# Attention and a squared-ReLU MLP on one core: first products by seven for more chunks, other loads of q and v, and a new written order

## The chip, the cores and the metric

The kernel runs on one core of one Trainium2 chip. The metric is device time in microseconds (us), from the start of the program to its end, as the median of several runs. One execution was also taken by the hardware profiler; its instructions, waits and transfers are the trace that is quoted here. Engines: PE (TensorE, matrix products; PEld is its weight load, which overlaps PE), DVE (VectorE), ACT (ScalarE), POOL (GpSimd), SP (SyncE, which here only issues transfers).

## The reference

For 8 batches and 8 heads, 576 tokens and head width 64, q attends to 16 beacon keys and then, causally, to k; the softmax times the values gives 64 columns a head. The 8 heads side by side are a token's 512 columns, and all 4608 tokens go through an MLP:

```python
scores = scale * np.matmul(q, k_all.transpose(0, 1, 3, 2))   # k_all: 16 beacons, then k; causal after them
a = np.exp(scores - max); a /= a.sum(-1, keepdims=True) + 1e-09
x = np.matmul(a, v_all)                  # -> 4608 x 512
h = x @ w_in                             # 512 x 2048
g = np.maximum(h, 0.0) ** 2
out = g @ w_out                          # 2048 x 512
```

## The kernel before

**Attention**, per batch of 576 tokens and pair of heads (pair p = 4 x batch + number). Batches 0 and 1 are loaded by GpSimd and turned by PE. From batch 2 on, q, k and v come in tiles of up to 128 tokens through SP's queue into six staging buffers `stg` as float32 (`ldBxC`: batch B, tensor x, tile C; `add_load`, lines 370 to 412), are cast by GpSimd (`castBxC`, line 342) into `qb`, `kb` (two buffers each in `qk_area`) or into the value tiles `vb`, and q and k are turned by one transposing transfer each (`trBq`, `trBk`, line 418) into `qT`, `kT`. In such a tile each partition holds one token of all heads, so pieces of 256 bytes are read. `qk...` (line 631) makes the scores of 512 columns at a time: in two PSUM pairs of banks (`strip`) and, where three pieces go together, in two of the four single banks `ps`. ACT takes the exponential into `pt` (`exp`, lines 653 and 729), DVE masks the diagonal blocks (`mask`, line 750, a minimum with `tri`), PE multiplies by the values with a column of ones (`av`, line 771), and DVE divides (`norm`, lines 788 and 790) into `xn`. `xn` is turned into `xT`, a ring of 1728 tokens: by PE for batches 0 to 2 (line 839), by transposing transfers on SP after that (`xt`, line 822).

**The MLP** works on nine chunks of 512 tokens. The first product (`s1.J...`) makes 2048 hidden rows of a chunk J in bf16 in `g[J % 2]`, the second (`s2.J...`) its 512 output columns.

- First product, chunks 0 to 6: 16 groups of 4 matmuls of 512 columns (line 1073), each drained by a relu on ACT or DVE (lines 1088, 1090), and squares in place by pairs of groups (`sq`, lines 1098, 1100). Where a chunk wraps in the ring (chunks 3 and 6), each matmul is cut in two.
- First product, chunks 7 and 8 (`BOTH = 7`, `add_first_both`, line 950): weights and tokens are cut into two halves each (even and odd tokens), and seven products of sums of the quarters take the place of eight (Winograd's scheme). GpSimd first copies the chunk out of the ring (`pull`), DVE makes the sums of the weights once (`asum`) and the differences of x per chunk (`xsum`, line 930). A PSUM bank pair runs through products 1, 6, 7 and 4; between them its content is copied to SBUF (`h...c1`, `u2`, `u3`), and DVE adds these copies to the other products (`c11`, `c22`, `c12`, line 997). Then come a relu in place and the square.
- Second product, chunks 0 and 1: plain, 128x512 (line 1123). Chunks 2 to 8: seven products (line 1182), with sums of g made by DVE (`sumJ.N.I`, line 1154) in three areas of `sum_area`, copies to `osb` (`ev`, line 340 or 342) and adds (line 1205). Results go out through SP.

**The order** of all this is not left to a scheduler: every operation is added to a list with its dependencies, and `SEQUENCE` (lines 16 to 147) names them one by one, with `@A`, `@D` or `@P` for the engine where there is a choice. Each engine runs its own operations strictly in that order, and PSUM banks, staging buffers and `held` areas are taken from pools as they come free. So an operation that waits holds up all that stands behind it on its engine.

Of the kernel before, what the change touches and what calls it, by code (L numbers as in the profile page):

```python
# [12 lines left out]
BIG = 3.0e38  # L13
# [3 lines left out]
ident tri fldq0 fldk2 fldq1 bkl0 fldq2 fldk1 warm sld0k1.0 fldk0 sld0q1.0 fcq0 sld0k1.2 tp0.0.0q eq0.0.0@D sld0q1.2  # L17
fck2 tpg0.0.0q fck3 tp0.0.2k fcq1 ld0v0 bkc0 tp0.0.3k ek0.0.2@A ek0.0.3@D tpg0.0.2k tpb0 tpg0.0.3k tp0.0.1q ekb0
fcq3@A fcq2@D ld0v1 bkl1 eq0.0.1@A tp0.0.3q fck1 tpg0.0.1q tp0.0.2q ld0v2 eq0.0.3@A eq0.0.2@D qk3.0.0 tpg0.0.3q ld0v3
tpg0.0.2q tp0.0.1k tp0.1.0k exp3.0.0 fck0 ld0v4 qk2.0.0 ek0.0.1@D ek0.1.0@D tpg0.0.1k tp0.0.0k exp2.0.0 win0 qk1.0.0  # L20
mask3.0.0 tpg0.1.0k tp0.1.0q ek0.0.0@A mask2.0.0 exp1.0.0 qk0.0.0 tpg0.0.0k win2 tp0.1.2k eq0.1.0@A mask1.0.0 exp0.0.0
ek0.1.2@D qk0.1.0 tpg0.1.0q tp0.1.1q tpg0.1.2k win1 exp0.1.0 mask0.0.0 qk0.1.1 cast0v0@D tp0.1.1k exp0.1.1 eq0.1.1@D
qk0.1.2 mask0.1.1 win3 tpg0.1.1q tp0.1.2q ek0.1.1@A cast0v1@D exp0.1.2 eq0.1.2@D qk1.1.0 tpg0.1.1k bkc1 av0.0.0
tpg0.1.2q av1.0.0 sld1k0.0 exp1.1.0 mask0.1.0 tp0.1.3k norm0.0.0 qk2.1.0 cast0v2 tpb1 ek0.1.3@D qk1.1.1 exp2.1.0 ekb1
cast0v3 av2.0.0 norm1.0.0 tpg0.1.3k xtp0.0.0 exp1.1.1 tp0.1.3q xte0.0.0@D qk1.1.2 sld1q0.0 eq0.1.3@D xtp0.0.1 av3.0.0
exp1.1.2 norm2.0.0 tpg0.1.3q qk3.1.0 cast0v4 norm3.0.0 xtp0.0.2 exp3.1.0 sld1k0.2 qk2.1.1 mask1.1.0 av0.1.0 mask1.1.1
mask2.1.1 exp2.1.1 sld1q0.2 mask3.1.1 av1.1.0 xte0.0.1@A norm0.1.0 ld1v0 xte0.0.2@A xtp0.0.3 mask2.1.0 qk2.1.2
xte0.0.3@A norm1.1.0 xtp0.1.0 exp2.1.2 s1.0.1.0 xte0.1.0@D s1.0.3.0 relu0.1.0@D qk3.1.1 ld1v1 relu0.3.0@A s1.0.11.0
exp3.1.1 av2.1.0 relu0.11.0@D mask3.1.0 xtp0.1.1 s1.0.0.0 norm2.1.0 xte0.1.1@A s1.0.2.0 relu0.0.0@D qk3.1.2 ld1v2
relu0.2.0@A sq0.0.0@D xtp0.1.2 sq0.1.0@A s1.0.6.0 xte0.1.2@D exp3.1.2 s1.0.8.0 relu0.6.0@D s1.0.9.0 relu0.8.0@D  # L30
s1.0.10.0 relu0.9.0@A av3.1.0 sq0.4.0@D relu0.10.0@A ld1v3 sq0.5.0@D s1.0.12.0 norm3.1.0 s1.0.4.0 relu0.12.0@A
s1.0.5.0 relu0.4.0@A ld1v4 tp1.0.0k relu0.5.0@A xtp0.1.3 sq0.2.0@A ek1.0.0 s1.0.13.0 s1.0.14.0 xte0.1.3@A relu0.13.0@D
wout0 tpg1.0.0k tp1.0.0q relu0.14.0@A sq0.6.0@D s1.0.11.1 eq1.0.0@D tp1.0.1k relu0.11.1@A s1.0.8.1 wout1 tpg1.0.0q
ek1.0.1 tp1.0.1q relu0.8.1@A qk4.2 tpg1.0.1k eq1.0.1@D tp1.0.2k wout2 exp4.2.0.0.0 s1.0.15.1 tpg1.0.1q ek1.0.2
tp1.0.3q exp4.2.1.0.0 s1.0.12.1 wout3 tpg1.0.2k eq1.0.3@D s1.0.5.1 relu0.12.1@A mask4.0.0 qk4.4 tpg1.0.3q relu0.15.1@A
relu0.5.1@D cast1v0 s1.0.2.1 exp4.4.0.0.0 tp1.0.2q cast1v1 relu0.2.1@D s1.0.14.1 eq1.0.2@D exp4.4.1.0.0 cast1v2
s1.0.13.1 relu0.14.1@D s1.0.0.1 tpg1.0.2q relu0.13.1@A cast1v3 mask4.0.2 mask4.0.1 qk5.7 sq0.7.1@A sq0.6.1@D cast1v4
relu0.0.1@A s1.0.1.1 exp5.7.-1.1.0 s1.0.9.1 relu0.1.1@D exp5.7.-1.0.0 av4.0.0 relu0.9.1@D exp5.7.1.0.0 s1.0.10.1
mask5.0.0 norm4.0.0 av4.0.1 relu0.10.1@A s1.0.7.1 sq0.4.1@A mask5.0.2 norm4.0.1 s1.0.3.1 sq0.5.1@A relu0.7.1@D
tp1.0.3k sq0.0.1@A xtp1.0.0 ek1.0.3 relu0.3.1@A s1.0.4.1 xte1.0.0@A s1.0.6.1 zero2 tpg1.0.3k relu0.4.1@D sq0.1.1@A  # L40
s1.0.15.0 wsum1 sq0.2.1@A s1.0.7.0 zero3 s2.0.0.0 relu0.15.0@A relu0.7.0@A relu0.6.1@D exp5.7.0.0.0 sq0.3.0@D s2.0.2.0
sq0.3.1@D sq0.7.0@D qk7.13 mask5.0.1 s2.0.0.1 exp7.13.-1.1.0 exp7.13.-1.0.0 av5.0.0 exp7.13.0.0.0 s2.0.0.2 norm5.0.0
ld2k0 exp7.13.1.0.0 wsum2 av5.0.1 s2.0.0.3 ld2q0 norm5.0.1 s2.0.3.0 ev0.0@A ld2q1 mask7.0.1 mask7.0.2 xtp1.0.1 ld2q2
s2.0.3.1 xte1.0.1@A cast2k0 ld2q3 s2.0.2.1 qk6.10 cast2q0 ld2k1 s2.0.2.2 exp6.10.0.0.0 cast2q1 ld2q4 s2.0.3.2
exp6.10.1.0.0 s2.0.2.3 exp6.10.-1.1.0 mask6.0.1 cast2q2 ld2k2 mask6.0.2 exp6.10.-1.0.0 s2.0.3.3 exp6.10.1.0.1 ev0.2@D
cast2q3 ld2k3 mask6.0.0 s2.0.1.0 ev0.3@A mask7.0.0 av6.0.0 cast2k1 st1 av7.0.0 norm6.0.0 ld2k4 cast2q4 s2.0.1.1
norm7.0.0 av6.0.1 cast2k2 tr2q av7.0.1 norm6.0.1 s2.0.1.2 norm7.0.1 cast2k3 xtp1.0.2 xtp1.0.3 xte1.0.2@D s2.0.1.3
xte1.0.3@A s1.1.1.0 ev0.1@A cast2k4 st0 s1.1.2.0 relu1.1.0@A tr2k s1.1.3.0 relu1.2.0@A s1.1.9.0 relu1.3.0@A sq1.1.0@D
s1.1.4.0 relu1.9.0@A s1.1.5.0 relu1.4.0@A ld2v0 s1.1.6.0 relu1.5.0@A sq1.2.0@D s1.1.13.0 relu1.6.0@A ld2v1 s1.1.14.0
ld2v2 relu1.13.0@A s1.1.15.0 relu1.14.0@A s1.1.8.0 relu1.15.0@A ld2v3 sq1.7.0@D qk8.2 relu1.8.0@A s1.1.10.0  # L50
exp8.2.0.0.0 sq1.4.0@D cast2v0 ld2v4 s1.1.11.0 relu1.10.0@D exp8.2.1.0.0 cast2v1 ld3k0 s1.1.0.0 relu1.11.0@A mask8.0.0
qk8.4 sq1.5.0@D relu1.0.0@A cast2v2 ld3q0 s1.1.7.0 exp8.4.0.0.0 sq1.0.0@D s1.1.12.0 cast2v3 ld3q1 exp8.4.1.0.0
# [155 lines left out]
def kernel(  # L208
# [694 lines left out]
    def add_first_both(j, G, sq):  # L903
# [32 lines left out]
        for half in range(2):  # L936
# [58 lines left out]
            def plus(name, chain, n, quad, added, u, last, half=half, bank=bank, done=done, ev=ev, keep=keep, sums=sums):  # L995
# [6 lines left out]
                if u:  # L1002
                    give.append(keep[added])
# [334 lines left out]
```

## Time and profile before

| what | value |
|---|---|
| median of 3 runs | 331.17 us (329.81 to 331.58) |
| span of the profiled execution, first to last instruction | 327.7 us |
| granted PE clock, mean | 1.000 |
| instructions in the trace | 8732 |
| matmuls of line 1073 / 1182 / 950 in the built order | 640 / 784 / 224 |

The profiled execution is given by its span; the times of the runs are whole device times, with a few microseconds around the span. In rows of a group, "x64 | 37.8, 599 | 16.9" means 64 instructions, busy 37.8 us in all, 599 ns a piece on average, and the engine idle for 16.9 us just before them, with what ended that. A matmul's own duration holds its passage through the pipeline; how fast PE really goes is read from the distance of starts, or from the chain, whose pieces (start, length, what) don't overlap. In a row of stretches stand the stretch, its length, the busy time of PE, PEld, DVE, ACT and POOL with counts, the granted clock, the share of the 16 DMA engines and GB/s.

### The profile page before, as it was taken

Reading aid. Unit: us, or ns where it says so; the run is one execution under the profiler, and the core shown is the slowest. Engines: PE = TensorE matmul, PEld = TensorE weight load, DVE = VectorE, ACT = ScalarE, POOL = GpSimd, SP = SyncE. Lnnn points to the kernel's source line nnn. Section 1 sums busy time; section 2 is a strip of 40 time slices with the busy share of each in tenths; the row PEclk is TensorE's granted clock in tenths of the full one; section 3 lists DMA queues with packets and bytes.
Section 4 is the critical chain, followed back from the end, with each engine's and each line's share of the span. In section 5 each row is a group of like instructions: output and inputs, shape, how many; then the busy total and the mean of one; then the engine's idle time right before and its main releaser. Section 6 shows DMA issues by size and latency. Waiting matters only on the chain.

```text
span 327.7 us, 8732 instructions
## 1 busy us (share of the span) xinstructions
PE 315.9 (96%) x3582; PEld 227.6 (69%) x3582; DVE 231.9 (71%) x487; ACT 225.7 (69%) x332; POOL 101.1 (31%) x149
## 2 busy tenths in 40 slices
PE   2999999999999999999999999999999999999995
PEld 1478785544565558888866565776788788888884
DVE  3777886534655899587864788768865797897871
ACT  4867796458874984777766889767837664695931
POOL 9854713404532450424033403641100252000000
PEclk9999999999999999999999999999999999999999
DMA  8999998899999999999999998997913210110033
GB/s 159 220 205 215 206 169 170 168 214 204 205 177 201 240 219 171 178 244 230 180 138 215 221 181 204 202 207 156 225 23 130 46 28 2 69 61 0 2 148 111
DMA packets 145602, 51.98 MB, mean 159 GB/s; under 512 B 132506, under 2 KB 140570, under 8 KB 145562
## 3 DMA queue, kind: packets, MB, share of 16 engines
q1 hardware_dynamic: 135901, 42.32, 65.7%
q0 software_dynamic: 8512, 8.49, 15.4%
q10 hardware_dynamic: 1149, 0.62, 0.9%
q8 instruction: 28, 0.46, 0.6%
q14 instruction: 12, 0.10, 0.1%
HBM read 37.22 MB, written 9.44 MB: 142 GB/s over the span
## 4 chain that ended last, share of the span: by engine, by line
PE 85%; DMA 8%; SPq 1%; ACT 1%; POOL 1%; DVE 1%; issue 1%; ACTq 0%; POOLq 0%; DVEq 0%
PE ps L1073 26%; PE ps L1182 21%; PE ps L771 9%; PE ps L1123 8%; PE strip L631 6%; PE strip L950 4%; PE ps L950 3%; DMA stg<-in_q_dram 3%; PE strip L1182 2%; DMA kT<-qk_area 2%; PE ps L631 2%; DMA osb<-in_q_dram 2%; DMA stg<-in_v_dram 2%; PE ps L839 1%; SPq L822 1%; PE ps L474 1%
## 5 line engine op out<-in xcount | busy, mean ns | idle before, releaser
L1073 PE MATMUL ps<-xT,w_in 128*128 128x512 bf16 (+6 forms) x640 | 106.3, 315 | 0.6 <-ACT pt L729 0.6
L1073 PEld LDWEIGHTS <-w_in 128*128 128x128 bf16 x640 | 56.2, 98 | 34.8 <-issue 1.6
L729 ACT ACTIVATE pt<-strip 128x1024 bf16<-128x1024 f32 (+3 forms) x77 | 69.6, 955 | 7.8 <-PE strip L631 7.7
L1088 ACT ACTIVATE g<-ps 128x512 bf16<-128x512 f32 (+2 forms) x82 | 44.4, 551 | 20.1 <-PE ps L1073 17.2
L342 POOL CAST qk_area<-stg 128x512 bf16<-128x512 f32 (+2 forms) x60 | 39.9, 672 | 53.7 <-DMA stg<-in_k_dram 31.5
L342 POOL CAST vb<-stg 128x512 bf16<-128x512 f32 (+1 forms) x38 | 27.4, 728 | 83.6 <-DMA stg<-in_v_dram 69.4
L750 DVE TENSOR_TENSOR pt<-pt,tri 128x512 bf16<-128x512 bf16 (+1 forms) x93 | 37.8, 424 | 16.1 <-ACT pt L729 14.8
L1182 PEld LDWEIGHTS <-g 128*128 128x128 bf16 x448 | 42.9, 98 | 7.0 <-issue 0.8
L771 PEld LDWEIGHTS <-pt 128*128 128x128 bf16 x930 | 35.8, 100 | 7.0 <-issue 1.2
L771 PE MATMUL ps<-vb,pt 128*128 128x65 bf16 x930 | 38.4, 197 | 0.0
L1182 PE MATMUL ps<-w_out,g 128*128 128x256 bf16 x304 | 38.0, 273 | 0.0
L1090 DVE TENSOR_SCALAR g<-ps 128x512 bf16<-128x512 f32 (+2 forms) x46 | 27.9, 607 | 13.2 <-PE ps L1073 12.6
L1182 PEld LDWEIGHTS <-sum_area 128*128 128x128 bf16 x336 | 32.0, 98 | 5.5 <-issue 1.4
L790 DVE TENSOR_TENSOR xn<-ps,rcp 128x320 bf16<-128x320 f32 (+2 forms) x64 | 31.5, 491 | 2.2
L340 ACT COPY osb<-ps 128x512 f32<-128x512 f32 x26 | 15.2, 586 | 25.2 <-PE ps L1182 19.0
L1123 PE MATMUL ps<-w_out,g 128*128 128x512 bf16 x128 | 31.2, 379 | 0.0
L1100 DVE TENSOR_TENSOR g<-g 128x1024 bf16<-128x1024 bf16 (+2 forms) x35 | 23.4, 673 | 10.6 <-ACT g L1088 9.9
L631 PEld LDWEIGHTS <-kT 64*128 64x128 bf16 x618 | 20.0, 95 | 14.1 <-issue 10.3
L631 PE MATMUL strip<-qT,kT 64*128 64x128 bf16 (+14 forms) x500 | 29.5, 246 | 0.3 <-ACT qT L340 0.2
L1098 ACT ACTIVATE g<-g 128x1024 bf16<-128x1024 bf16 (+2 forms) x29 | 26.7, 941 | 3.0 <-DVE g L1090 2.0
L729 ACT ACTIVATE pt<-ps 128x512 bf16<-128x512 f32 x42 | 23.4, 599 | 5.7 <-PE ps L631 5.6
L1182 PE MATMUL ps<-w_sum,sum_area 128*128 128x256 bf16 x208 | 26.0, 273 | 0.0
(93 smaller groups left out, 357.7 us busy)
## 6 DMA issues: line engine op xcount, KB each, us to landing
out_dram<-osb SPq DMA_DIRECT2D x16, 512.0 KB, 3.8
stg<-in_q_dram SPq DMA_DIRECT2D x24, 256.0 KB, 4.6
stg<-in_k_dram SPq DMA_DIRECT2D x18, 256.0 KB, 5.1
stg<-in_v_dram SPq DMA_DIRECT2D x18, 256.0 KB, 4.6
w_in<-in_moe_w_in_dram POOLq DMA_DIRECT2D x4, 512.0 KB, 12.0
w_out<-in_moe_w_out_dram POOLq DMA_DIRECT2D x4, 512.0 KB, 10.9
stg<-in_v_dram POOLq DMA_DIRECT2D x6, 256.0 KB, 8.0
stg<-in_k_dram SPq DMA_DIRECT2D x6, 224.0 KB, 4.1
```

The lines of the kernel that those rows point to most:

```text
L342: eng[e].tensor_copy(dst, src)
L631: nc.tensor.matmul(out, kT[b % 2][hp, pr, 128 * c:128 * c + 128], rhs, start=True, stop=True)
L729: nc.scalar.activation(out, in_, AF.Exp, bias=0.0, scale=scale)
L750: nc.vector.tensor_tensor(out=d, in0=d, in1=tri[0:rows, m0:m0 + m, 0:w][:, None].to_broadcast([rows, 2, m, w]), op=ALU.min)
L771: nc.tensor.matmul(a[:, at + (t - tl[0]) * (D + 1):at + (t - tl[0] + 1) * (D + 1)], P[0:rr, hj, o:o + 128], vb[b % 2][0:rr, c, 2 * pr + hj ...
L790: nc.vector.tensor_tensor(out=xn[b % 2].rearrange("p t (h d) -> p h t d", d=D)[:, h0:h0 + nh, tl[0]:tl[0] + nt], in0=a[:, :, :, 0:D], in1= ...
L1073: nc.tensor.matmul(h[:, lo - spans[0][0]:hi - spans[0][0]], w_in_sb[:, mc, ft * 128:(ft + 1) * 128], xT[:, mc, lo % RING:lo % RING + hi - lo],
L1088: nc.scalar.activation(dst, h, AF.Relu, bias=0.0, scale=1.0)
L1090: nc.vector.tensor_scalar(out=dst, in0=h, scalar1=0.0, scalar2=None, op0=ALU.max)
L1098: nc.scalar.activation(d, d, AF.Square, bias=0.0, scale=1.0)
L1123: nc.tensor.matmul(o, G[:, fc, ts * 128:(ts + 1) * 128], w_out_sb[:, fc, :], start=(fc == 0), stop=(fc == NFT - 1))
L1182: nc.tensor.matmul(o, lhs[:, f, t * 128:(t + 1) * 128], rhs[:, f], start=fresh and f == 0, stop=f == HF - 1, skip_group_check=True)
```

## The change

- **Chunks 3 to 6 by seven products too** (`BOTH = 3`). The form is another: four units of two row groups each, every bank chain in single `ps` banks; x is read in place from the ring, every other column, without pulls; of the four differences of x, three stand in a small area `spare` and one replaces its operand in the ring. The relu is folded into the adds, by a custom DVE instruction (`TENSOR_ADD_SAT` with bounds 0 and BIG), and into the drain of product 4. The areas that hold the copies are three, in `spare`.
- **The sums of the second product** are made mostly in place in g (`sum 2`, `sum 4` wait for products 1 and 2), with one area `s_sum`; GpSimd may make them.
- **q of batches 2 to 7** is loaded for two heads at a time with four consecutive tokens to a partition (pieces of 1 KB), so that the columns of `qT` come out in another order, and the scores read them with a step of 128, cut at column 512.
- **v of batches 2 to 7** is loaded by GpSimd's queue with a cast straight into `vb`, without staging and without a cast instruction.
- **One buffer** instead of two for `qb` and for `kb`; a cast waits for the transpose of the batch before.
- **Masks** may be made by GpSimd (a select of the diagonal block), casts by ACT or DVE; `tri` is smaller, `bks` lies in `w_sum`.
- A relu now waits for the second product two chunks back, where its matmuls did.
- **A new `SEQUENCE`** throughout, from the first loads on.

```diff
-    FAST, FAST_PE = 2, 0.9
-    BOTH = 7
-    NSTG, NPT, RB = 6, 3, 3
+    FAST, BOTH = 2, 3
+    SOFT = "v"
+    NSTG, NPT, RB, NH = 6, 3, 3, 3
...
+    def add_soft_load(b, x, c, behind):
...
+            insts.append(nc.gpsimd.dma_start(out=dst[lo:rows], in_=t[b, :, t0:t0 + rows - lo, :].transpose([1, 0, 2])))
...
+            if fours:
+                return [queue.dma_start(out=st[0:rows].rearrange("p (u s) d -> p u s d", s=4),
+                                        in_=t[b, 2 * c:2 * c + 2, 0:4 * rows, :].rearrange("u (p s) d -> p u s d", s=4))]
...
+            if b >= NPE:
+                fours = qT[b % 2][hp, pr, 0:512].rearrange("p (s n) -> p n s", s=4)
+                parts = [(x, y, z) for x, y, z in ((t0, min(t1, 512), fours), (max(t0, 512), t1, None)) if x < y]
...
+                if e == "POOL":
+                    for i in range(m):
+                        nc.gpsimd.affine_select(out=d[:, :, i], in_=d[:, :, i], compare_op=ALU.is_ge, fill=0.0,
+                                                base=Nb if m0 + i == 0 else 0, pattern=[[0, 2], [1, w]], channel_multiplier=-1)
+                    return
...
+        def in_ring(c, q):
+            return [xT[:, HM * c:HM * c + HM, lo % RING:lo % RING + hi - lo].rearrange("p m (i q) -> p m q i", q=2)[:, :, q]
+                    for lo, hi in spans]
...
+        for n, o, a, c in ((1, pieces(s[1]), b12, b11), (2, pieces(s[2]), b22, pieces(s[1])), (3, b12, b22, b12),
+                           (4, pieces(s[4]), b21, pieces(s[2]))):
...
+                for i in range(2):
+                        f = 2 * u + i
+                        for part, (at, w) in zip(rhs, where):
+                            for m in range(HM):
+                                nc.tensor.matmul(o[:, i * HT + at:i * HT + at + w], lhs[:, m, f * 128:(f + 1) * 128],
+                                                 part[:, m], start=fresh and i == 0 and at == 0 and m == 0, stop=m == HM - 1,
+                                                 skip_group_check=True)
...
+                    nc.vector._custom_dve(TENSOR_ADD_SAT, out=dst, in0=bank_of(chain),
+                                          in1=held[keep[added].held[1]].rearrange("p (f t) -> p f t", f=2), s0=BIG, s1=0.0)
...
+            product(2, "z", A[0, 1], b21, cuts, feeds + weights)
+            product(1, "x", A[0, 0], b11, cuts, feeds + weights)
+            hold("c1", 1)
+            plus("c11", "z", 2, block(0, 0), "c1", True)
+            product(5, "y", a_sum[1], [s[1]], one, a_ops[1] + x_ops[1])
+            product(6, "x", a_sum[2], [s[2]], one, a_ops[2] + x_ops[2] + ev["c1"])
+            hold("u2", 6)
+            product(7, "x", A[1, 0], b12, cuts, a_ops[3] + x_ops[3] + ev["u2"])
+            hold("u3", 7)
+            plus("c22", "y", 5, block(1, 1), "u3", False)
+            product(4, "x", A[1, 1], [s[4]], one, x_ops[4] + ev["u3"])
+            last("c21", 4, block(1, 0))
+            product(3, "y", a_sum[4], b22, cuts, a_ops[4] + ev["c22"])
+            plus("c12", "y", 3, block(0, 1), "u2", True)
```

585 lines of the change are left out of this document (285 added, 300 removed).

## The prediction

> **What bounds the kernel now.** I read the page's busy times first, then the busy times of engines by stretch, then the chain that ended last, then the groups by shape.
>
> ```profile
> span 327.7 us, 8732 instructions
> PE 315.9 (96%) x3582; PEld 227.6 (69%) x3582; DVE 231.9 (71%) x487; ACT 225.7 (69%) x332; POOL 101.1 (31%) x149
> ```
>
> ```profile
> 0.00:16.00 16.00, 9.23 (x94) 4.54 (x95) 8.38 (x28) 9.88 (x18) 14.31 (x27) 1.00 1.05 190
> 105.00:262.00 157.00, 155.87 (x1872) 112.38 (x1871) 118.76 (x243) 115.33 (x165) 45.64 (x67) 1.00 0.94 180
> 280.00:300.00 20.00, 20.00 (x186) 17.94 (x184) 18.13 (x34) 14.81 (x17) 0.00 (x0) 1.00 0.14 53
> ```
>
> Columns: stretch, its length, busy PE, PEld, DVE, ACT, POOL, granted clock, DMA share, GB/s. From 105 to 262 us, where chunks 2 to 6 are worked, PE lacks 1.1 of 157 us at clock 1.00; DVE is 76% busy, ACT 73%, POOL 29%. DMA is at 0.94 there, yet PE hardly waits for it, having other products to do. From 280 to 300 DVE is 91% busy (18.13 of 20) and PE still full. A full PE row isn't by itself PE at its peak, so the spacing of the products decides, from the chain:
>
> ```profile
> 68.46 9.50 PE ps L1073 x44
> ...
> 288.54 1.75 PE strip L950 x16
> ...
> 309.06 4.37 PE ps L1182 x40
> ```
>
> A 128x512 product costs 9.50/44 = 0.216 us, a 128x256 one 1.75/16 = 0.109, and both run back to back. The kernel is bound by PE's work, so a change pays if it takes work from PE and the other engines keep up.
>
> **The change, part by part.** The sum is made against the profiled span of 327.7 us; the median of the runs, 331.17, lies 3.5 above it, and I assume that difference stays.
>
> *Seven products in chunks 3 to 6.* The first product of a chunk was 16 x 4 products of 512 columns, 64 x 0.216 = 13.8 us. It becomes 4 units x 7 products x 4 matmuls of 256 columns, 112 x 0.109 = 12.2 us: 1.6 us less, **-6.4 us** for four chunks. Rows of line 950 show this form at that price already, for chunks 7 and 8. Chunks 3 and 6 wrap in the ring, so 64 matmuls of each are cut in two; two halves of 0.109 against one whole of 0.216 put an extra instruction at 2 ns, 128 x 2 ns = **+0.3**.
>
> *Columns read with a step.* The products now read every other column of xT itself, and the scores of batches 2 to 7 read columns 128 apart. The first occurs nowhere before; batch 0's first scores read columns 120 apart:
>
> ```profile
> 8.79 0.53 PE L631 MATMUL strip<-qT,kT 64*128 64x240 bf16 x4 [0.25 <-ACT qT L340]
> 9.25 0.80 PE L474 MATMUL ps<-ident,qk_area 120*128 120x120 bf16 x8
> ...
> 12.66 0.53 PE L631 MATMUL strip<-qT,kT 64*128 64x336 bf16 x4
> 13.12 0.49 PE L474 MATMUL ps<-ident,qk_area 112*64 112x112 bf16 x6
> ```
>
> Four matmuls with step (368 columns a head) hold PE 0.46 us from start to next start, four without (416 columns) 0.46 too. I take nothing; a gain is excluded, since columns without a step already run at PE's price. At half speed, 64 matmuls in each of six chunks would cost 64 x 6 x 0.109 = 42 us more: the upper end, kept as a rival.
>
> *More score matmuls.* Segments are cut at column 512: in the built order 846 against 618.
>
> ```profile
> 77.89 0.61 PE L631 MATMUL strip<-qT,kT 64*128 64x240 bf16 x10
> 78.43 2.76 PE L1073 MATMUL ps<-xT,w_in 128*128 128x512 bf16 x12
> ...
> 85.46 0.63 PE L631 MATMUL strip<-qT,kT 64*128 64x16 bf16 x16
> 86.02 1.04 PE L1123 MATMUL ps<-w_out,g 128*128 128x512 bf16 x4
> ```
>
> Ten matmuls over two banks hold PE 0.54 us, sixteen 0.56, so one more costs 3.3 ns: 228 x 3.3 ns = **+0.8**.
>
> *Handing a bank on.* Each unit sends one bank through products 1, 6, 7 and 4, with a copy to SBUF between.
>
> ```profile
> 314.34 0.37 ACT L340 COPY osb<-strip 128x256 f32<-128x256 f32 x1 [1.05 <-PE strip L1182]
> ```
>
> ```profile
> 313.26 1.04 PE L1182 MATMUL strip<-w_out,g 128*128 128x256 bf16 x8
> 314.14 1.04 PE L1182 MATMUL ps<-w_sum,sum_area 128*128 128x256 bf16 x8
> ```
>
> A copy starts 0.20 us after PE goes on (314.14 to 314.34). With 0.586 for the copy (below) and about 0.1 back, estimated from the half of that delay, PE needs 0.89 us of other work. In the written order 29 of the 72 handings in chunks 3 to 8 have two units of 0.437 between (0.87) or barely more, one has a single one. So 28 x 0.03 + 0.45 = **+1.3**, if the copying engine is free.
>
> *Engines' work from 105 to 262.* Counted in the written order from chunk 2's first product to chunk 7's, by these rows:
>
> ```profile
> L1088 ACT ACTIVATE g<-ps 128x512 bf16<-128x512 f32 x64 | 37.8, 599 | 16.9 <-PE ps L1073 14.5 <-DVE rcp L788 1.9
> ...
> L1098 ACT ACTIVATE g<-g 128x1024 bf16<-128x1024 bf16 x21 | 21.9, 1055 | 2.9 <-DVE g L1090 2.0 <-DVE pt L750 0.4 <-DVE rcp L788 0.2
> L340 ACT COPY osb<-ps 128x512 f32<-128x512 f32 x26 | 15.2, 586 | 25.2 <-PE ps L1182 19.0 <-PE ps L1123 5.3 <-DMA out_dram<-osb 0.8
> ```
>
> ```profile
> L750 DVE TENSOR_TENSOR pt<-pt,tri 128x512 bf16<-128x512 bf16 x62 | 29.5, 478 | 11.8 <-ACT pt L729 10.5 <-ACT pt L653 1.1
> ...
> L1090 DVE TENSOR_SCALAR g<-ps 128x512 bf16<-128x512 f32 x32 | 22.0, 688 | 10.8 <-PE ps L1073 10.5
> ...
> L997 DVE TENSOR_TENSOR g<-ps,stg 128x512 bf16<-128x512 f32 x16 | 10.7, 684 | 3.4 <-PE ps L950 3.4
> ...
> L1154 DVE TENSOR_TENSOR sum_area<-g 128x1024 bf16<-128x1024 bf16 x14 | 10.2, 731 | 0.3
> ...
> L750 DVE TENSOR_TENSOR pt<-pt,tri 80x160 bf16<-80x160 bf16 x31 | 9.7, 315 | 4.3 <-ACT pt L729 4.3
> ```
>
> DVE: 48 adds at 0.684 (+32.8); 21 holds and last relus against 30 relus (-9 x 0.688 = -6.2); 15 differences of xT at no more than 0.684 (+10.3); 8 casts, bounded by the same (+5.5); 6 squares and 5 sums (11 x 0.731 = -8.0) and 26 + 15 masks (-12.4, -4.7) gone. Net +17.3: 118.8 becomes **136**, 90% of the 150.6 us that PE's work leaves of 157. ACT: 43 holds and relus at 0.59 more, 42 relus at 0.599 less, 6 squares at 1.055 and 10 casts at 0.59 more: +12.4, 115.3 becomes **128** (85%). In the stretch from 280 to 300 DVE ran at 91% with PE full, so I cost this at nothing, narrowly. If that cover fails, every us that DVE is short in this stretch is a us of the total. The adds are now a custom instruction with relu folded in, which no row shows: from below 0.684, since the same operands move as in line 997's adds; from above a second pass over the bank, 0.688 more, 72 x 0.688 = 50 us of DVE, which would bind. I take 0.684, the nearest row.
>
> *GpSimd.* It gets masks, 7 sums, 5 differences and the loads of v that cast; it loses 20 casts of v, 23 of q and k, and 4 pulls.
>
> ```profile
> L342 POOL CAST qk_area<-stg 128x512 bf16<-128x512 f32 x48 | 32.5, 680 | 43.8 <-DMA stg<-in_k_dram 24.6 <-DMA stg<-in_q_dram 18.8
> L342 POOL CAST vb<-stg 128x512 bf16<-128x512 f32 x30 | 22.1, 747 | 76.2 <-DMA stg<-in_v_dram 65.8 <-PE ps L631 9.9 <-PE strip L631 0.5
> L386 POOL DMA_DIRECT2D stg<-in_v_dram x10 | 8.6, 862 | 7.3 <-DMA w_in<-in_moe_w_in_dram 4.4 <-DVE rcp L788 1.6 <-DMA qk_area<-in_k_dram 1.0
> ...
> L327 POOL TENSOR_SCALAR_AFFINE_SELECT tri<-tri 128x128 bf16<-128x128 bf16 x4 | 1.0, 296 | 0.1
> ```
>
> Gone: 20 x 0.747 + 23 x 0.680 + 4 x 0.73 (a pull is a copy of 512 elements as the casts are) = 33.5 us. Added: 24 load issues x 0.862 = 20.7; 67 selects, each of one to two times the 0.296 row, 20 to 40; 12 sums and differences, whose nearest row is a copy (below) at 0.6 to 3.5, taken 1.5: 18. So 45.6 becomes 91 to 111 of 151 us: more than half, with waits. A load of v waits on POOL's queue for the previous but one batch's av, and the masks behind it wait too; their av is what PE would miss. Cover: scores and products of the next chunk.
>
> *Loads of q* in 1 KB runs, 30 v loads off SP's queue, but one buffer each for q and k where there were two: a cast now waits for the previous batch's transpose.
>
> ```profile
> qT<-qk_area SPq DMA_TRANSPOSE x6, 6.6
> ```
>
> Ten casts of 0.68 and two such landings take 20 us of a period of some 30, so I cost it at nothing. PE's 1.1 idle us of the stretch may go with lighter DMA; I take half, **-0.6**.
>
> *The start.* q of pair 0 is now issued behind q of pairs 2 and 3 and the table load:
>
> ```profile
> 0.81 1.52 ACTq L538 DMA_DIRECT2D osb<-in_q_dram  x3
> ...
> 2.36 1.28 ACT L554 ACT_TABLE_LOAD   x1 [2.36 <-issue]
> ```
>
> That is 1.52/3 + 1.28 = 1.8 us later, while pair 3's q comes earlier by two issues (1.0). I take the difference, **+0.8**; ends 0 and 1.8.
>
> Sum: -6.4 + 0.3 + 0.8 + 1.3 - 0.6 + 0.8 = **-3.8**: span 323.9, time **327.4 us**. What follows PE's last product (an add and a store) has the same instructions in both.
>
> **Rivals.** (1) *The vector engines' queue eats the gain.* At 90% and 85% each is a queue in fixed order: an add that waits for a late product holds up the copy behind it, and that copy PE's next product. If DVE gets no further than 87% (between the 91% above and the 83% of 30.84 in 37 us here),
>
> ```profile
> 105.00:142.00 37.00, 37.00 (x447) 25.59 (x446) 30.84 (x63) 26.90 (x41) 12.96 (x19) 1.00 1.13 198
> ```
>
> the stretch takes 136/0.87 = 156 us, nearly as before: with the small terms outside it about 331. (2) *GpSimd and DVE hold each other up: slower.* What the two do to each other shows here:
>
> ```profile
> L342 POOL COPY pt<-xT x4: 612/938/3544, 266.4 to 271.2; 128x512 bf16<-128x512 bf16 x4
> ```
>
> ```profile
> L1154 DVE TENSOR_TENSOR sum_area<-g x14: 676/688/1097, 125.7 to 312.9; 128x1024 bf16<-128x1024 bf16 x14
> ```
>
> Minimum, median and maximum: a POOL copy went from 0.61 to 3.54 us beside DVE's sums, a DVE sum from 0.68 to 1.10. With POOL past half its time a mask or sum on it comes 1 to 3 us late, and av or product 6 behind it stands in PE's fixed order. From four such misses of 1 us net the gain is gone, from six the kernel is slower; of 53 masks, sums and differences on it in the stretch, 1 us at every fourth costs 13 and gives 327.4 + 13 = 340. [...]
>
> [...]
>
> (3) *The stepped columns are read at half speed*: 42 us, 369 us.
>
> **How the numbers follow.** Forecast, PE stays the bound: 0.52, its own range 323.5 (all of -7.5, no costs) to 329.4. Rival 1: 0.18 (329.5 to 332.8). Rival 2: 0.27 (333 to 346). Rival 3: 0.03. A measurement of this kernel tells about 0.5% (1.7 us) from no change. Faster 0.52, same 0.18, slower 0.30. The range reaches from 322 to 338: outside lie the upper third of rival 2, rival 3 and a twentieth below.
>
> **What would show it.** Right: chunks 3 to 6 at 0.109 us a matmul, PE full from 105 us on with DVE near 90%, the custom adds near 0.68 us. Wrong: gaps on PE released by copies or adds (rival 1), by masks or sums on POOL (rival 2), or products of xT spaced 0.2 us (rival 3); adds far over 0.68 us.

## The result, and the profile after

The changed kernel takes 367.12 us (365.62 to 369.73, four runs) against 331.27 (329.81 to 331.58, four runs): ratio 1.111, 95% interval 1.105 to 1.117. It is 36 us **slower**; 327.4 was predicted, with 338 as the upper end. Medians here are over all executions of a run; ratios leave out the few that came out more than 1.5% above the fastest of their kernel.

The page of the profiled execution (365.62 us), first line, engines, and the chain that ended last by engine and line:

```profile
span 363.9 us, 9707 instructions
PE 350.4 (96%) x3988; PEld 249.3 (69%) x4002; DVE 247.4 (68%) x488; ACT 222.8 (61%) x338; POOL 163.8 (45%) x246
...
PE 87%; DVE 6%; DMA 3%; issue 2%; SPq 1%; ACT 1%; DVEq 0%
PE ps L1217 19%; PE ps L1008 18%; PE strip L679 15%; PE ps L1111 12%; PE ps L1160 8%; PE ps L824 7%; PE ps L679 4%; PE strip L1217 2%; DVE g L1046 2%; DMA osb<-in_k_dram 2%; DVE xn L843 1%; DMA xT<-xn 1%; PE ps L892 1%; DVE spare L984 1%; PE ps L515 1%
```

The same stretches as before, columns as before:

```profile
105.00:262.00 157.00, 154.95 (x1819) 108.62 (x1820) 114.59 (x216) 106.02 (x152) 68.46 (x109) 1.00 0.81 135
280.00:300.00 20.00, 19.34 (x273) 15.48 (x270) 14.46 (x31) 12.94 (x19) 5.34 (x9) 1.00 0.21 65
```

PE is as full as before, at clock 1.00, and has 34 us more to do; DVE and ACT lost share in the stretch (119 to 115, 115 to 106 us). So it is not waiting that grew: PE itself got slower. Line 679 (the scores, line 631 before) holds 19% of the chain, where it held 8% (6% and 2%, the same part of the page before):

```profile
PE ps L1073 26%; PE ps L1182 21%; PE ps L771 9%; PE ps L1123 8%; PE strip L631 6%; PE strip L950 4%; PE ps L950 3%; DMA stg<-in_q_dram 3%; PE strip L1182 2%; DMA kT<-qk_area 2%; PE ps L631 2%; DMA osb<-in_q_dram 2%; DMA stg<-in_v_dram 2%; PE ps L839 1%; SPq L822 1%; PE ps L474 1%
```

With the unrounded shares that is 0.187 x 363.9 - 0.081 x 327.7 = 41.5 us more. Three pieces of the chain after (start, length, what), and the same shape of matmul after and before:

```profile
73.10 1.68 PE strip L679 x14
...
77.48 1.61 PE strip L679 x18
...
82.62 1.53 PE strip L679 x22
```

```profile
L679 PE MATMUL strip<-qT,kT 64*128 64x240 bf16 x64 | 17.2, 513 | 0.0
```

```profile
L631 PE MATMUL strip<-qT,kT 64*128 64x240 bf16 x64 | 9.1, 282 | 0.2 <-ACT qT L340 0.2
```

A two-bank visit was 0.54 us (prediction, ten matmuls at 77.89) and is 1.68: three times as long, with four matmuls more. The scores ask for the same products; what changed is that they read columns of `qT` 128 apart (256 bytes).

### The profile page after: what moved, and what is told of

The parts are those of the page before. It is cut to its first block, busy times and chain, and to the rows that moved or that the text cites. A ratio compares the mean times of both kernels' runs of the same rounds, so it can differ in the third digit from the quotient of the medians.

```text
span 363.9 us, 9707 instructions
## 1 busy us (share of the span) xinstructions
PE 350.4 (96%) x3988; PEld 249.3 (69%) x4002; DVE 247.4 (68%) x488; ACT 222.8 (61%) x338; POOL 163.8 (45%) x246
## 3 DMA queue, kind: packets, MB, share of 16 engines
q0 software_dynamic: 37504, 12.13, 30.8%
## 4 chain that ended last, share of the span: by engine, by line
PE 87%; DVE 6%; DMA 3%; issue 2%; SPq 1%; ACT 1%; DVEq 0%
PE ps L1217 19%; PE ps L1008 18%; PE strip L679 15%; PE ps L1111 12%; PE ps L1160 8%; PE ps L824 7%; PE ps L679 4%; PE strip L1217 2%; DVE g L1046 2%; DMA osb<-in_k_dram 2%; DVE xn L843 1%; DMA xT<-xn 1%; PE ps L892 1%; DVE spare L984 1%; PE ps L515 1%
## 5 line engine op out<-in xcount | busy, mean ns | idle before, releaser
L800 POOL TENSOR_SCALAR_AFFINE_SELECT pt<-pt 128x256 bf16<-128x256 bf16 (+1 forms) x98 | 36.7, 398 | 92.7 <-ACT pt L777 91.1
L1217 PEld LDWEIGHTS <-g 128*128 128x128 bf16 x672 | 64.2, 98 | 10.6 <-issue 2.6
L1046 DVE CUSTOM_DVE_ANT_0 g<-ps,spare 128x512 bf16<-128x512 f32 x72 | 48.7, 687 | 24.4 <-PE ps L1008 16.4
L679 PE MATMUL strip<-qT,kT 64*128 64x128 bf16 (+13 forms) x652 | 61.3, 327 | 0.4 <-DVE qT L349 0.4
L347 ACT COPY spare<-ps 128x512 f32<-128x512 f32 x51 | 29.7, 588 | 32.1 <-PE ps L1008 26.7
L1111 PE MATMUL ps<-xT,w_in 128*128 128x512 bf16 (+2 forms) x251 | 45.6, 325 | 0.3
L1008 PE MATMUL ps<-xT,w_in 128*128 128x256 bf16 (+4 forms) x384 | 42.5, 247 | 0.7 <-DMA xT<-xn 0.7
L1008 PEld LDWEIGHTS <-qk_area 128*128 128x128 bf16 x320 | 27.7, 97 | 8.0 <-issue 3.4
L1186 POOL TENSOR_TENSOR g<-g 128x1024 bf16<-128x1024 bf16 x11 | 24.7, 2253 | 18.6 <-DVE g L1186 11.6
L1072 ACT ACTIVATE g<-g 128x1024 bf16<-128x1024 bf16 x31 | 32.1, 1058 | 1.6 <-DVE g L1046 1.5
```

The costliest lines, as they stand in the source:

```text
L347: nc.scalar.copy(dst, src)
L679: nc.tensor.matmul(out, kT[b % 2][hp, pr, 128 * c:128 * c + 128], rhs, start=True, stop=True)
L800: nc.gpsimd.affine_select(out=d[:, :, i], in_=d[:, :, i], compare_op=ALU.is_ge, fill=0.0, base=Nb if m0 + i == 0 else 0, pattern=[[0, 2], ...
L1008: nc.tensor.matmul(o[:, i * HT + at:i * HT + at + w], lhs[:, m, f * 128:(f + 1) * 128], part[:, m], start=fresh and i == 0 and at == 0 and ...
L1046: nc.vector._custom_dve(TENSOR_ADD_SAT, out=dst, in0=bank_of(chain), in1=held[keep[added].held[1]].rearrange("p (f t) -> p f t", f=2), s0= ...
L1072: nc.scalar.activation(both, both, AF.Square, bias=0.0, scale=1.0)
```

## The experiments

**Theory**: the step in the columns that the scores read makes the loss. **Rivals**: the vector engines' queue, GpSimd and its transfers, the seven products. Ratios are to the kernel before on the same chip, with 95% intervals.

| run | us | ratio |
|---|---|---|
| changed, q by tiles of 128 tokens | 335.23 | 1.014 (1.010 to 1.019) |
| before, q four tokens to a partition | 370.21 | 1.125 (1.120 to 1.129) |
| changed, step in the write | 339.68 | 1.028 (1.025 to 1.030) |
| before, q by fours, step in the write | 342.39 | 1.036 (1.033 to 1.039) |
| before, v by GpSimd's transfers | 342.78 | 1.037 (1.034 to 1.040) |
| step in the write, sums on DVE | 353.52 | 1.068 (1.065 to 1.072) |
| changed, columns put in order by copies | 341.28 | 1.034 (1.030 to 1.037) |
| the same, copies on GpSimd | 341.07 | 1.033 (1.030 to 1.036) |
| q by tiles, v by casts again | 351.76 | 1.064 (1.059 to 1.069) |
| step in the write, v by casts again | 354.48 | 1.073 (1.069 to 1.077) |
| q by tiles, no loads of v | 326.81 | 0.993 (0.990 to 0.996) |
| q by tiles, no GpSimd masks | 336.52 | 1.019 (1.011 to 1.028) |
| q by tiles, neither | 327.43 | 0.995 (0.991 to 0.999) |
| changed, columns as they lie | 328.81 | 0.998 (0.994 to 1.001) |

**Undo the step; do it alone.** First the changed kernel without it, then the kernel before with that part of the change alone (load, step and cut at column 512).

```diff
-            t0, rows = (0, 128) if fours else (512, S - 512)
+            t0, rows = 128 * c, min(128, S - 128 * c)
```

> The changed kernel with one part undone: q of batches 2 to 7 is loaded as before, 128 tokens to a tile in pieces of 256 bytes, so its columns lie in the order of tokens and the scores read them without a step and without the cut at column 512. Theory A (score matmuls read columns 256 bytes apart at about 1.7 ns a column instead of 0.42): the two-bank visits fall from 1.6 to 0.55 us, the span falls by about 41 us, time 323 to 329. Theory B (queues of DVE, ACT and GpSimd hold PE up; the step matters little): time stays above 350. Theory C (both): 330 to 345.

```diff
+                fours = qT[b % 2][hp, pr, 0:512].rearrange("p (s n) -> p n s", s=4)
```

> The kernel before with that part alone: q of batches 2 to 7 four tokens to a partition, scores read with a step of 128 columns and cut at column 512; all else, the order too, as before. Theory A: PE's score rows grow by about 41 us, time 366 to 374 (a little less if lighter loads help). Theory B: time 328 to 335.

Undone: 335.23. Alone: 370.21. The chain of the kernel before with the step alone:

```profile
77.82 1.68 PE strip L647 x14
82.19 1.61 PE strip L647 x18
```

These are the visits of the changed kernel to the hundredth. Summed from each start to the next, without listed waits, the scores take 31.0 us before, 72.7 after and 72.1 here, 41.1 more than before; the span grew by 40.2 (327.7 to 367.9). The step is the whole of that part's cost. But the changed kernel without it is still 1.4% above the one before, so there is a second question.

**What a step costs.** Two runs of one execution each, with a different step in each batch; the scores of these batches are of other tokens, and only their durations count.

> The changed kernel, where each batch reads its first 512 columns of q with another step, so that the scores are of other tokens than they should be; the number, width and order of matmuls and the cut at column 512 stay. Batch 2: no step; 3: 256 columns (512 bytes); 4: 132 (264 bytes); 5: 160 (320 bytes); 6: 64 (128 bytes); 7: 128 (256 bytes, as changed). Read off: ns a column by the durations of score matmuls of one width. If the cuts cost: batch 2 as slow as 7. If a power of two collides: 4 and 5 fast, 3, 6 and 7 slow at 1.7 ns. If any far step costs: all but batch 2 at about 1.7 ns a column. Time 330 to 368 by this.

> As the other kernel of mixed steps, with near ones: batch 2 a step of 2 columns (4 bytes), 3: 4 (8 bytes), 4: 8 (16 bytes), 5: 16 (32 bytes), 6: 32 (64 bytes), 7: 120 (240 bytes, the step of batch 0's first scores in both kernels). Scores are of other tokens than they should be. If each column's own fetch costs once columns no longer share a line of some width, the time per column jumps from 0.42 to 1.7 ns between two of these batches; 4 bytes stays at 0.42, since products of xT with that step take 275 ns against 272. If only 256 bytes collides, all six stay at 0.42, batch 7 too. Time 325 to 350.

By batch, from groups by shape in the batch's own window; the first fence is from the first of these runs (no step, cut at 512), the others are from the second (4, 8, 16 bytes):

```profile
L693 PE MATMUL strip<-qT,kT 64*128 64x240 bf16 x8 | 1.1, 264 | 0.0
```

```profile
L693 PE MATMUL strip<-qT,kT 64*128 64x240 bf16 x8 | 1.1, 267 | 0.0
...
L693 PE MATMUL strip<-qT,kT 64*128 64x240 bf16 x8 | 1.5, 382 | 0.0
...
L693 PE MATMUL strip<-qT,kT 64*128 64x240 bf16 x8 | 2.4, 594 | 0.0
```

| columns read with a step of | 64x240, ns | 64x400, ns | ns a column (400 less 144 columns) |
|---|---|---|---|
| none (2 bytes) | 264 | 330 | 0.42 |
| 4 bytes | 267 | 337 | 0.45 |
| 8 bytes | 382 | 510 | 0.82 |
| two distant places in turn | 388 | 535 | 0.93 |
| 16 to 320 bytes, four places or more | 570 to 600 | 824 to 872 | 1.6 to 1.7 |

From 16 to 320 bytes the size of the step no longer matters, powers of two or not (264, 320, 240 bytes): 1.6 to 1.7 ns a column, four times the price of columns that lie together (0.42). At 4 bytes the price is nearly that without a step (0.45), at 8 about twice that (0.82), at 16 the full price. Two distant places in turn cost 0.93 and not the full price.

**Move the step from the read to the write.**

```diff
-                    out, rhs = out.rearrange("p (n s) -> p n s", s=ns), view[:, x // ns:y // ns]
+                        out = out.rearrange("p (n s) -> p s n", s=ns)
+                        rhs = view.rearrange("p n s -> p s n")[:, :, x // ns:y // ns]
```

> The changed kernel whole, with one edit in the scores of batches 2 to 7: the columns of qT are read in the order in which they lie (four runs without a step), and the step of four columns goes to the place in PSUM to which the product is written. Theory A (only a step in the operand that is read costs; a step of 16 bytes in what is written costs nothing): the two-bank visits come back from 1.67 to 0.55-0.62 us and the three-bank ones from 2.4 to 0.8-0.9, and since PE's other work in the changed kernel is 277.7 us against 279.8 before and its idle time 5.3 against 8.0, the time is 322 to 328. Theory B (the steps of writing cost as those of reading): visits of 1.6 and 2.4, time 355 to 370. Theory C (the step in writing is free, but the rest of the change is late once PE runs faster, as in the run with q loaded by tiles): visits of 0.6, time 329 to 338.

> The kernel before with q of batches 2 to 7 loaded four tokens to a partition, as in the run that cost 41 us, but with the step in the write to PSUM and not in the read. Theory A (writing with a step is free): 327 to 332, the lighter loads being worth 0 to 3 us and the cut of one matmul in two at token 512 costing 0 to 2. Theory B: 365 to 372 as with the step in the read.

> One look at the price of a step in what the scores write to PSUM, by batch; the scores of these batches are of other tokens, so only durations count. Batch 2 reads four runs and writes without a step; batches 3 to 6 read without a step and write with steps of 2, 4, 8 and 16 columns (8, 16, 32, 64 bytes); batch 7 writes two halves in turn. Theory W (the step in the write is what costs in the run with the step moved there, 372 ns for 64x240 against 282): batch 2 at 280, batch 3 between 280 and 372, batch 4 at 372, batches 5 and 6 at 372 or more. Theory R (the four runs of the read cost, not the write): batch 2 at 372, batches 3 to 6 at 280. Batch 7 is left open: two places in turn cost 388 to 396 in the read.

339.68 and 342.39: between the theories. A visit is 0.92 us, neither 0.55 nor 1.68:

```profile
73.50 0.92 PE strip L683 x14
```

The third run (one execution, 336.83 us) says why: four runs read and no step written give 263 ns, every step written from 8 to 64 bytes gives 383 to 390, two halves written in turn 380. So a step in the write to PSUM costs too, and at 8, 16, 32 and 64 bytes the same (64x400 takes 497 ns at each of these, 330 without a step written):

```profile
L689 PE MATMUL strip<-qT,kT 64*128 64x400 bf16 x2 | 0.5, 497 | 0.0
```

In the kernel before with q by fours and the step in the write, the scores take 45.1 us, 14.1 more than before, and the span is 13.2 longer (340.9): the lighter loads of q by themselves bring 0.9 us at most.

**What stands between the rest and the kernel before: v's transfers.**

```diff
-            queue = nc.sync                       # v of batches 2 to 7, then 30 casts
+            insts.append(nc.gpsimd.dma_start(out=dst[lo:rows], in_=t[b, :, t0:t0 + rows - lo, :].transpose([1, 0, 2])))
```

> The kernel before with v of batches 2 to 7 cast by GpSimd's transfers into its tiles, and nothing else changed; the casts' 30 places in the order are left out. Theory A (this part is neutral: the casts were beside other work, and so are the transfers): 328 to 333. Theory B (with q in 256-byte pieces the transfers of v on a second queue crowd those of q and k, as in the run with q by tiles, where one transpose of kT took 12 us and PE stood 4.8 us): 333 to 340, with PE's idle time up by 4 or more.

342.78: 12 us more by this part alone. What PE waits for (us, times, longest), and the transposes' time from issue to landing, 5.9 us before (second number: this run):

```profile
PE strip L655 <- DMA kT<-qk_area: 7.9, 3, 3.7
```

```profile
kT<-qk_area SPq DMA_TRANSPOSE x6, 5.9
```

```profile
kT<-qk_area SPq DMA_TRANSPOSE x6, 11.7
```

With q in 256-byte pieces the transfers of v on GpSimd's queue crowd the transposes of k; these land 6 us later at the median and PE stands for three of them, 7.9 us in all. Each of the three stops cost more than its length: the granted clock is at half for 3.4 us behind it. One of them:

```profile
140.70:144.00 3.30, 3.30 (x19) 2.26 (x16) 0.42 (x1) 1.91 (x2) 0.61 (x1) 0.50 0.49 99
```

By estimate 3 x 3.4 us at half the clock, with PE at half its pace there (the next trace shows this), cost PE another 5.1 us; with the stops that is 13.0, where the span grew by 12.3 (327.7 to 340.0). So the two account for this part's whole loss. The trace of the run with q by tiles (337.56 us; its executions lie between 331.7 and 337.9) shows one such stop, 4.8 us long, and what follows:

```profile
119.73 12.06 DMA kT<-qk_area
131.79 0.05 issue
131.84 1.03 PE strip L679 x9
132.87 0.94 PE ps L824 x15
```

```profile
132.00:136.00 4.00, 4.00 (x46) 3.06 (x43) 1.28 (x3) 1.94 (x2) 0.00 (x0) 0.50 0.05 9
```

There the clock is at half for 6.8 us, 4.5 of them behind the stop; 15 products with v take 0.94 us at this clock, 0.46 at 110.64 ahead of the stop. So stop and clock together cost about 7 us (4.8 + 2.3, by the same estimate).

Putting v's casts back was meant to show it from the other side, with q by tiles and with q by fours:

```diff
-    SOFT = "v"
+    SOFT = ""                                     # and 30 words castBvC@P in SEQUENCE
```

> The changed kernel with q loaded in 128-token tiles as before and v of batches 2 to 7 loaded by SP and cast by GpSimd as before (30 casts put back in GpSimd's order some ten places behind their loads), so that of the change the seven products, their sums and the new order are left. Theory A (the transfers of v crowd those of q and k, as in the kernel before with that part alone, 342.8): PE no longer stands for a transpose of kT, and the time is 324 to 331, below the 335.2 of the run with q by tiles. Theory B (the seven products' sums and additions make DVE and GpSimd late, and 30 more casts of 0.7 us on GpSimd make it worse): 336 to 346.

> The run with q four tokens to a partition and the step in the write (339.7 us), with v of batches 2 to 7 loaded by SP and cast by GpSimd as before. Theory A (with q in 1 KB pieces there is room on the DMA queues, so v's transfers cost nothing there and GpSimd's 30 casts only load it): 339 to 346. Theory B (v's transfers cost there too): 330 to 338.

351.76 and 354.48, but these two tell nothing of v's transfers: my places for the casts were too early, and GpSimd stood for v's landing in front of its masks (the first of the two):

```profile
POOL vb L211 <- DMA stg<-in_v_dram: 57.9, 13, 12.0
```

So the work was left out instead: v's loads, GpSimd's masks, both. The outputs of these three are of another v or without those masks.

```diff
-            insts.append(nc.gpsimd.dma_start(out=dst[lo:rows], in_=t[b, :, t0:t0 + rows - lo, :].transpose([1, 0, 2])))
-                        nc.gpsimd.affine_select(out=d[:, :, i], in_=d[:, :, i], compare_op=ALU.is_ge, fill=0.0,
```

> The run with q by tiles (335.2 us) without the 36 loads of v of batches 2 to 7 (the products then read the v of the batches 0 and 1): neither their bytes on the queue nor the 29 us of GpSimd that issue them. Theory A (v's transfers crowd the loads and transposes of q and k): the 4.8 us for the transpose of batch 4's k go, and the time is 325 to 330. Theory B (the seven products with their sums and additions, or the masks on GpSimd, are late by themselves): 333 to 337.

> The run with q by tiles without the 100 masks that GpSimd makes (these probabilities stay unmasked); v is loaded as changed. Theory A (v's transfers are the cause, GpSimd's masks are on time): 333 to 337. Theory B (the masks come late behind GpSimd's sums and transfers and hold up the products with v): 325 to 331.

> Both left out: GpSimd has its casts and its 22 sums only, 66 us less. If either the transfers of v or GpSimd's lateness is what stands between the run with q by tiles and the kernel before, this is 320 to 327, near what PE's own work gives (310.9 us of PE, 7 idle at the start, 8 behind the last matmul). If it stays at 330 or more, the seven products' chain of holds, additions and sums on ACT and DVE sets the rate.

326.81, 336.52, 327.43. Without v's loads about 7 us go (by the ratios, 1.014 against 0.993); without masks nothing goes, with or without v. The kT transposes land in 4.9 us without v's loads (7.1 with), and PE waits 0.2 us for one; in the run without masks PE still stands 3.5 us for a kT, and the clock stays at 0.50 for 5.8 us behind it.

```profile
kT<-qk_area SPq DMA_TRANSPOSE x6, 4.9
```

GpSimd's own load is not it: both left out takes it from 162 us to 97 and gives the same time as v left out. Leaving v out takes away 29 us of issuing on GpSimd as well, but the masks' 37 us, which stand in the same queue, were worth nothing. It also takes v's bytes off the DMA engines altogether, so this run is no fair forecast of the rest of the change; that the second queue does the harm is shown by the kernel before with that part alone, where the same v is loaded.

**GpSimd's sums.**

```diff
-sum3.1.0@P
+sum3.1.0@D                                        # and 21 more
```

> The run with the step in the write, and the 22 sums that GpSimd makes (2.2 us each for the gates' sums) handed to DVE in the same places of the order. Theory A (GpSimd's sums cost nothing where they stand, DVE has 22 sums of 0.5 to 0.75 us more, 14 us): 0 to 5 us longer than that run. Theory B (GpSimd's sums come late or hold up DVE's operations beside them, 2.35 us for one cast of 0.6): 2 to 6 us shorter than that run.

353.52, 14 us longer than with the sums on GpSimd. PE then waits for DVE (adds, sums) and once 4.6 us for a kT:

```profile
PE ps L683 <- DMA kT<-qk_area: 4.6, 1, 4.6
PE ps L1012 <- DVE g L1050: 3.3, 6, 1.2
...
PE ps L1221 <- DVE g L1190: 1.9, 1, 1.9
```

The clock stays at 0.50 for 4.8 us behind this stop, so that about 7 of the 14 us (4.6 + 2.4, estimated as above) lie at this one transpose; why it came late was not followed, and the sums' own price on DVE stays open. That GpSimd's sums hold DVE up (theory B) fell all the same: nothing was gained.

**Is there a gain without the step?** First a version that computes the whole: five copies per batch put the columns in order.

```diff
+                        copy_on(e, qT[1][:, pr, 0:512].rearrange("p (n s) -> p n s", s=4),
+                                qT[0][:, pr, 0:512].rearrange("p (s n) -> p n s", s=4))
```

> The changed kernel with one step more: the transposed q of a batch lands as before in one tile, and five copies (one to each pair of heads and one for the last tokens, one on DVE, one on ACT, three on GpSimd) put its columns into the order of the tokens in a second tile, from which the scores then read without a step and uncut. Theory A (the step in the scores was the whole loss, and PE sets the end): visits of 0.55 and 0.8; PE's other work 277.7 us with 31 of scores, 5 to 9 idle and 8 to 9 behind the last matmul, so 323 to 328, below the kernel before. Theory B (what the rest of the change saves on PE is lost in waits when PE runs faster, or the 30 copies come late): 329 to 336.

> The same with all five copies of each batch on GpSimd, in the same places. Theory A (the copies hide beside PE on any engine): within 1 us of the run with the mixed engines. Theory B (GpSimd is late with its masks already, and 12 more copies of 0.7 to 1.5 us hold up the scores behind them): 2 to 8 us longer.

341.28 and 341.07. The scores are back at 30.8 us, but in the first of the two PE waits 5.3 us for a copy that waits for the transpose on its engine's queue, the clock is at 0.50 for 3.4 us behind the longest of these stops, and PE is idle elsewhere; the rest of this loss I did not take apart.

```profile
PE strip L554 <- DVE qT L211: 5.3, 3, 3.8
```

Then the step alone taken away: the scores read the columns as they lie, so that they are of other tokens.

```diff
-            if b >= NPE:
-                fours = qT[b % 2][hp, pr, 0:512].rearrange("p (s n) -> p n s", s=4)
```

> The changed kernel whole (q in 1 KB pieces, v by GpSimd's transfers, the new order), but its scores read the columns of qT in the order in which they lie, without step, cut or copy; they are then scores of other tokens, and only the time counts. Theory A (v's transfers cost only where q comes in 256-byte pieces; with the light loads the rest of the change saves what its spans show once the scores' excess is taken off: 363.9 - 41.9 = 322.0 and 338.0 - 14.5 = 323.5): time 322 to 327. Theory B (what the rest saves is only there while PE is slow; at PE's full rate v's transfers, sums or masks are late also with the light loads): 329 to 341, with PE idle 12 us or more beside the start and the end.

328.81, ratio 0.998 (0.994 to 1.001): no difference that can be told from the kernel before, between the two theories. Page and stretch:

```profile
span 326.3 us, 9265 instructions
PE 310.6 (95%) x3774; PEld 237.8 (73%) x3774; DVE 246.9 (76%) x488; ACT 220.5 (68%) x338; POOL 160.4 (49%) x246
```

```profile
105.00:262.00 157.00, 151.57 (x2062) 124.97 (x2061) 135.90 (x258) 121.95 (x178) 76.80 (x125) 1.00 0.92 146
```

PE's busy time fell by 5.3 us (315.9 to 310.6), the span by 1.4: 3.9 came back as idle PE, almost all in this stretch (157 - 151.6 = 5.4, against 1.1 before), with DVE at 136 of 157 us. What PE waits for behind the start, the longest:

```profile
PE ps L1005 <- DVE xT L981: 1.2, 2, 0.8
PE strip L676 <- DMA qT<-qk_area: 1.0, 1, 1.0
PE ps L676 <- DVE osb L1237: 1.0, 1, 1.0
```

It waits for no transpose of k, though these land in 7.2 us at the median here, as late as in the run with q by tiles (7.1); the latest takes 8.5, there 12.1. Beyond the scores, the rest of the change is worth less the faster PE goes, in the three traces that show it: spans less the scores' own excess give 5.5 us with the step in the read (36.2 longer, scores 41.7 more), 3.9 with the step in the write (10.3 and 14.2) and 1.1 without (1.4 shorter, scores 0.3 less). No version that computes the whole was below the kernel before.

## Why the prediction was wrong

- **Failed: "Columns read with a step ... I take nothing."** The runs put the read step of the scores at 41 to 42 us (41.1 alone, 41.7 in the changed kernel). The row behind this term was batch 0's first scores. It misled twice. There the step goes between two places only, which costs 388 ns for 64x240, not 570. And PE was slow there anyway: the same kernel's columns without a step, by shape, from 8 to 16 us and from 40 to 64 us:

```profile
L631 PE MATMUL strip<-qT,kT 64*128 64x336 bf16 x4 | 0.9, 452 | 0.1
```

```profile
L631 PE MATMUL strip<-qT,kT 64*128 64x336 bf16 x4 | 0.6, 301 | 0.0
```

  A matmul without a step takes 452 ns there for what later takes 301, so "four with step as fast as four without" was true of that stage alone: 64x240 with the step took 401 there, 64x208 and 64x256 without one 351 and 417. The row was quoted with its time, 8.79 us, and the argument used it for 60 to 270 us.
- **Rival 3** had the size (42 us, 369) by coincidence, and the wrong place and chance. It put half speed on xT's products, whose step is 4 bytes; these nearly keep their price (0.45 against 0.42 ns a column in the runs with mixed steps). The scores, whose step is 256 bytes, got none of it.
- **Seven products, -6.4 + 0.3, and handing a bank on, +1.3**: the mechanism holds, at little more than half the size. Summed from each start to the next, without listed waits, the first products of chunks 3 to 6 take 56.3 us before and 52.0 after; those of chunks 7 and 8, which were by seven already but in another form, take 24.5 and 26.2. With chunks 0 to 2 (43.2 and 43.0) that is 124.0 and 121.2: 2.8 us less, where these terms give 4.8. Two things stand against it. A product that reads the ring, with a step of 4 bytes, takes 0.114 us from start to start at the median; one that reads the differences in `spare`, which lie together, takes 0.109, line 950's price. The starts of four products each show it (0.46, 0.43 and 0.46 us):

```profile
204.41 0.61 PE L1008 MATMUL ps<-xT,qk_area 128*128 128x256 bf16 x4
204.87 0.60 PE L1008 MATMUL ps<-spare,qk_area 128*128 128x256 bf16 x4
205.30 0.62 PE L1008 MATMUL ps<-xT,w_in 128*128 128x256 bf16 x4
205.76 0.62 PE L824 MATMUL ps<-vb,pt 128*128 128x65 bf16 x15
```

  By estimate that is 384 x 5 ns = 1.9 us over the six chunks. The rest is 28 late starts of 0.03 to 0.3 us, most of them where one product or visit ends, 2.8 us in all. The +0.3 was no difference: in the kernel before, 128 products of chunks 3 and 6 are cut in two as well.
- **The custom add** at 0.684: right.

```profile
L1046 DVE CUSTOM_DVE_ANT_0 g<-ps,spare 128x512 bf16<-128x512 f32 x72 | 48.7, 687 | 24.4 <-PE ps L1008 16.4 <-ACT spare L347 5.8 <-PE ps L824 1.5
```

- **Engines' work**: DVE 136 us in the stretch was predicted, 135.9 is what it does there at PE's full rate (87%, the share at which rival 1 let it bind); GpSimd is 76.8 there. The prediction's 91 to 111 was an error of addition: its own terms (45.6 - 33.5 + 20.7 + 20 to 40 + 18) give 71 to 91, and so rival 2's "more than half" was too sure. ACT 128 was a little high, 122.
- **Rival 1** (331, 0.18) comes nearest to what is left without the step (328.8): PE's saving goes back into waits, most of those listed for DVE, some for transfers. **Rival 2** (340, 0.27) failed in its mechanism: masks left out change nothing, and with the sums taken from GpSimd the kernel is slower. What GpSimd was shown to cost is in its transfers, where q is loaded in 256-byte pieces. I had counted *loads of q and v* at nothing and -0.6; alone on the kernel before, the first costs 40 us (by the step in the scores) and the second 12.
- **The cut** at column 512, +0.8: small as put; with the cut and no step a visit of 14 takes 0.55 where one of 10 took 0.54. **The start**, +0.8: wrong in sign; the first scores start at 7.25 us, before at 8.79. PE also comes to full rate earlier. 24 products with v hold it for 0.73 us from start to start at 18.16 us in the changed kernel; before, 48 of them hold it for 2.63 at 21.59, 1.32 for 24:

```profile
18.16 0.90 PE L824 MATMUL ps<-vb,pt 128*128 128x65 bf16 x24
18.89 0.27 PE L892 MATMUL ps<-ident,xn 112*128 112x112 bf16 x2
```

```profile
21.59 2.82 PE L771 MATMUL ps<-vb,pt 128*128 128x65 bf16 x48
24.22 0.37 PE L839 MATMUL ps<-ident,xn 112*128 112x112 bf16 x2
```

  In the run without the step, products with v, PE's own turns and scores take 72.8 us from start to start, before 76.2. So of PE's 5.3 us less, by this estimate, some 3.4 come from the earlier full rate and only 2.4 from first products by seven. (The second products take 0.7 more.)

Slow instructions of the kind on which rival 2 rests are in the trace of the changed kernel too (one DVE cast, 0.42 us at the median, took 2.35 beside a GpSimd sum of 2.50); that the kernel's time hangs on them, no run shows.

## What to carry to other kernels

A layout that makes loads cheaper can be paid for where PE reads it (here 41 us for a step of 256 bytes): look at the innermost step of the moving operand before counting bytes of DMA. Take the price of a form from a row in the stage where it will run; a row from the start, where PE was slow anyway (452 ns for what later took 301), can hide the whole price. And when a part moves work to another queue, ask which transfers it meets there: v's transfers cost 7 to 12 us beside q in 256-byte pieces. Beside q in 1 KB pieces PE waited for no transpose of k in the one trace at full rate, but no run here compares with and without them there. Ask what a stop of PE costs beyond its length: behind stops of 1.9 to 4.8 us the clock was at half for 3.4 to 5.8 us more, though behind one of 2.0 it stayed at 1.00.

## What the runs showed of the hardware

- PE's price for columns read from SBUF, in the scores: 0.42 ns lying together, 0.45 at a step of 4 bytes, 0.82 at 8, 1.6 to 1.7 at the steps from 16 to 320 bytes. A write to PSUM with a step of 8 to 64 bytes makes 64x400 take 497 ns against 330, at each of the four steps (8, 16, 32, 64).
- At the start PE takes 1.5 times as long for the same matmul (64x336: 452 ns against 301), until 24.4 us in the kernel before and 16.6 in the changed one. The traces hold no clock record ahead of these moments, and where there is none the views print 1.00; so the mean of 1.000 for the kernel before says nothing of its first 24 us. PE's row was 94% busy or more from 8 to 24 us there; what ends the slow stage was not shown.
- Later drops do show in the clock row. Behind stops of 3.7, 2.3 and 1.9 us (the kernel before with v by GpSimd's transfers) the clock is 0.50 for 3.4 us each; around one of 4.8 (q by tiles) for 6.8, 4.5 of them behind it. Not every stop does it: behind one of 2.0 us in the run without masks it stays at 1.00.
- GpSimd's sum of 128x1024 bf16 takes 2.25 us, DVE's 0.69 to 0.76; a copy of 128x512 bf16 with a step of 256 bytes takes 0.81 us on DVE and 1.10 on ACT, on average, and the 30 copies on GpSimd, 6 of which are shorter, take 1.06.
